# Splitting q and k for two heads at a time, and V once per unit, in a float16-split attention kernel

## The chip, the cores and the metric

The kernel runs on one core of a Trainium2 chip. The metric is the time of one execution on the device in microseconds. The engines named are PE (TensorE matmul; PEld is its weight load), DVE (VectorE), ACT (ScalarE), POOL (GpSimd) and SP (SyncE, which here only issues DMAs).

## The reference

Banded attention with a distance bias is followed by a two-layer feed-forward block (FF) on the same tokens. A query sees the 8 global keys and the 96 keys up to and including its own.

```python
# q, k, v: 4 batches, 8 heads, 768 tokens, 64 wide
scores = np.matmul(q, k.transpose(0, 1, 3, 2)) / np.sqrt(D)
keep = is_global | is_local            # key < 8, or 0 <= rel < 96
scores = np.where(keep, scores - slopes * dist, -1e9)
a = softmax(scores)
x = (a @ v) -> (3072, 512)
h = x @ w_in                           # 512 -> 2048
g = np.maximum(h, 0) + alpha * np.minimum(h, 0)
out = g @ w_out                        # 2048 -> 512
```

## The kernel before

The 3072 tokens are cut into 12 units `u` of 256 tokens, three to a batch. The first unit of a batch looks at three blocks of 128 keys, the others at four: for each of a unit's two query blocks its own 128 keys, and a far block of the 96 keys ahead of it and 32 leading keys of the batch. So the score window of a query block is 256 keys wide, and 128 for the first block of a batch. `windows` lists them.

Attention of unit `u` runs while the FF of the unit or two ahead of it uses PE. Units 0 to 2 attend in float32 (`plain`), while the weights are loaded and split. From unit 3 on every operand is split into a float16 high part and a float16 remainder. `mul` makes the high part (on ACT, DVE or POOL, as the planner chooses), `rest` makes the remainder (on DVE). For each head `attend` does this:

- one DMA brings `raw`, 128 partitions of q, k and V, 928 columns (736 in the first unit of a batch). The 64 rows of q and of k stand in it twice, in partitions 0 to 63 and again in 64 to 127 (L612).
- `q2` holds q's high part above and its remainder in the lower 64 partitions, `khi` and `klo` hold k's two parts, each twice (L622 to L625). So the two products of 128 rows at L656, `q2` with `khi` and `q2` with `klo`, sum all four cross terms.
- `vhi` and `vlo` split the head's V blocks (L631 to L641), far blocks included.
- DVE adds the bias `D` and takes a maximum (L662), ACT takes the exponential (L667), ACT or DVE and DVE split the probabilities into `ps` (L713, L714), an SP DMA transposes them into `pt` (L718), and PE multiplies them with V (L733), for two heads one behind the other.

FF of unit `u` and slice `f` (16 slices): twelve products of 256 columns into PSUM `h` (L795), activation on ACT and DVE into `g` (L343, L816, L818, L367), then per token block three products of 512 columns into `o` (L835). After the last slice ACT scales `o` into `os` (L842), an SP DMA stores it, and the two `o` buffers serve the next unit.

The order of instructions is fixed when the kernel is built. `Plan` keeps every operation with a key (its due slot), a cost and its buffers, runs a list schedule with the slots that `BUFS` gives to each tag, and emits the operations in the order of their planned start. On the chip each engine, SP's queue too, runs its own list strictly in that order. One FF slice is one step of the key. Scores of a head have the key of its place, the splits of q and k stand `KP` = 2 ahead of it, those of V one behind. `raw`, `q2`, `khi` and `klo` have two buffers each, PSUM `sp` and `h` have two.

Of the kernel before, what the change touches and what calls it, by code (L numbers as in the profile page):

```python
# [15 lines left out]
F16 = mybir.dt.float16  # L16
# [7 lines left out]
P = 128  # L24
# [22 lines left out]
def lay_out(q, k, v, n_global, n_local, moe_w_in, moe_w_out, moe_alpha):  # L47
# [6 lines left out]
    qk = np.zeros((2, 4, P, 672), q.dtype)  # L54
    vw = np.zeros((2, P, H * 256), q.dtype)
    for u in range(NU):
# [32 lines left out]
        "in_qkv_dram": qkv,  # L89
        "in_first0_dram": np.concatenate([qk[0, :, :, :544], vw[0, :, : H * 192].reshape(P, 4, 384).transpose(1, 0, 2)], axis=2),  # L90
        "in_first1_dram": cont(qk[1]),
        "in_first1v_dram": cont(vw[1].reshape(P, 2, 1024).transpose(1, 0, 2)),
# [200 lines left out]
NPLAIN = (8, 8, 8)  # L293
# [11 lines left out]
PT4 = 0  # L305
DL = 3
PREQ = (2,)
PREV = (2,)
PREP = (2,)
# [6 lines left out]
VLEAD = 22  # L316
# [3 lines left out]
BUFS = dict(rw=17, raw=2, q2=2, khi=2, klo=2, vhi=3, vlo=3, pr=2, sm=6, pt=2, ps=2, xn=1, xt=2, g=3, gh=3, gl=3,  # L320
# [3 lines left out]
def fast(tc, cn, a):  # L324
    nc = tc.nc
    ctx = ExitStack()
    with ctx:
# [218 lines left out]
        def load_first(u, h, key):  # L546

            x = buf("rw", f"first{u}_{h}", [P, 1024])
            nk, n = (672, 672) if u else (544, 928)

            def load():
                nc.sync.dma_start(out=x.t[:, :n], in_=a["first1" if u else "first0"][h // 2])
                if u == h == 0:
                    cn["load_alpha"]()
# [31 lines left out]

        def attend(u, h, key):

            b, c = divmod(u, 3)
            nk = 416 if c else 288  # L590
            nb = 4 if c else 3
            nv, npr = 64 * nb, 128 * nb
            plain = u < 3 and h < NPLAIN[u]
            uh = f"{u}_{h}"

            kp = key - KP
            if plain:

                if u < 2:
                    q2, qk_ = first[u, h]  # L600
                    rv, vrt = firstv[u, h]
                else:
                    q2 = rv = buf("raw", "raw" + uh, [P, 928])
                    op("SP", kp - 4, c_dma(P * 4 * (256 + nk + nv)), lambda: nc.sync.dma_start(
                        out=q2.t[:, : 256 + nk + nv], in_=a["qkv"][u, :, h, : 256 + nk + nv]), w=[q2])
                    qk_ = lambda: q2.t[:64, : 256 + nk]
                    vrt = lambda: q2.t[:, 256 + nk : 256 + nk + nv]
                q_ = lambda: qk_()[:, :256]
                keys = [(q2, lambda: qk_()[:, 256:])]
            else:  # L610
                raw = buf("raw", "raw" + uh, [P, 928])
                op("SP", kp - 4, c_dma(P * 4 * (256 + nk + nv)), lambda: nc.sync.dma_start(  # L612
                    out=raw.t[:, : 256 + nk + nv], in_=a["qkv"][u, :, h, : 256 + nk + nv]), w=[(raw, 0), (raw, 1)])
                rq, rv = (raw, 0), (raw, 1)
                rawt = lambda: raw.t
                vrt = lambda: raw.t[:, 256 + nk : 256 + nk + nv]
                q2 = buf("q2", "q2_" + uh, [P, 256], F16)
                q_ = lambda: q2.t
                khi = buf("khi", "khi" + uh, [P, 416], F16)
                klo = buf("klo", "klo" + uh, [P, 416], F16)  # L620
                kk = lambda: rawt()[:, 256 : 256 + nk]
# [4 lines left out]
                if (u, h) == (3, 0):  # L626
                    for x in range(H):
                        op("POOL", kp, c_pool(384, 1), lambda x=x: nc.gpsimd.tensor_scalar(
                            out=Dh[x].t, in0=Dh[x].t, scalar1=QS * QS, scalar2=None, op0=ALU.mult), w=[Dh[x]])
                keys = [(khi, lambda: khi.t), (klo, lambda: klo.t)]  # L630
            if not plain:  # L631
                vhi = buf("vhi", "vhi" + uh, [P, 256], F16)
                vlo = buf("vlo", "vlo" + uh, [P, 256], F16)
                vv = lambda: vrt()[:, :nv]
                if u in PREV:
                    mul(kp + 3, vv, vv, vs[b], [vs[b]], [rv], "ACT", nv)
                    copy(kp + 3, lambda: vhi.t[:, :nv], vv, [rv], [vhi], nv)
                    rest(kp + 3, lambda: vlo.t[:, :nv], vv, None, lambda: vhi.t[:, :nv], [rv, vhi], [vlo], nv, "POOL")
                else:
# [3 lines left out]
            sp = buf(idle(u, h, "sp", "h"), "sp" + uh, [P, 512])  # L643
# [7 lines left out]
            def scores():  # L651
                if (u, h) == (1, 0):
                    keep_busy(sp.t)
                for qb, off, n, _, pc in windows(u):
                    for j, (_, kk) in enumerate(keys):
                        nc.tensor.matmul(sp.t[:, pc : pc + n], lhsT=q_()[:, 128 * qb : 128 * qb + 128],  # L656
                                         rhs=kk()[:, off : off + n], start=j == 0, stop=j == len(keys) - 1)

            cost = (2 * npr * 0.84 if plain else 0.852 * npr)
            op("PE", key, cost, scores, r=[q2] + [x for x, _ in keys], w=[sp])  # L660
# [26 lines left out]
            if plain:  # L687
# [11 lines left out]
                prods = lambda: ((pt.t, vrt()),)  # L699
                used = [pt, rv]  # L700
                cost = 207 * nb
            else:
                ps = buf("ps", "ps" + uh, [P, 2, 512], F16)
                pt = buf("wf" if PT4 and u > 2 else "pt", "pt" + uh, [P, 2, 512], F16)
# [3 lines left out]
                if u in PREP:  # L708
                    mul(key + 2, pp, pp, PSC, [], [pr], "ACT", npr)
                    copy(key + 2, p0, pp, [pr], [(ps, 0)], npr)  # L710
                    rest(key + 2, p1, pp, None, p0, [pr, (ps, 0)], [(ps, 1)], npr, "POOL")
                else:
                    mul(key + 2, p0, pp, PSC, [pr], [(ps, 0)], "ACT", npr)  # L713
                    rest(key + 2, p1, pp, PSC, p0, [pr, (ps, 0)], [(ps, 1)], npr)  # L714
# [7 lines left out]
                prods = lambda: ((pflat(), vhi.t), (pflat(), vlo.t), (pflat()[:, npr:], vhi.t))  # L722
# [324 lines left out]
```

## Time and profile before

| | |
|---|---|
| median of 3 runs | 657.1 us (656.23 to 658.21) |
| the profiled execution | 655.59 us, of which the span is 653.8 us |
| PE busy | 624.0 us of the span (95%) |
| DVE, ACT, POOL busy | 518.0, 406.8, 129.1 us |
| granted TensorE clock | 0.997 over the span |
| DMA | 92.9 MB moved, 63.1 MB of it read from HBM |

The matmul records overlap and their ends are modelled, so that a PE which is called busy may still lose time. What a product costs is therefore read from one start to the next.

### The profile page before, as it was taken

The numbers are of one execution on the slowest core, as the hardware profiler recorded it, in microseconds if no ns is written. First come the engines' busy times: TensorE is split into PE (matmuls) and PEld (weight loads), VectorE is DVE, ScalarE is ACT, GpSimd is POOL, SyncE is SP. The second block draws the span as 40 slices with busy tenths as digits, with TensorE's granted clock in tenths as the row PEclk, the third lists the DMA queues.
The fourth block names the chain that finished last, engine by engine and source line by source line (L and its number), as shares of the span: only waits on it lengthen the run. The fifth ranks groups of instructions, "written<-read, shape, count | busy, mean of one in ns | idle before, by whom it ended". The sixth has DMA issues, their size and how long they took to land.

```text
span 653.8 us, 13833 instructions
## 1 busy us (share of the span) xinstructions
PE 624.0 (95%) x4964; PEld 438.0 (67%) x4964; DVE 518.0 (79%) x1497; ACT 406.8 (62%) x1085; POOL 129.1 (20%) x185
## 2 busy tenths in 40 slices
PE   8998998999999999899899999999899999999995
PEld 7785666675666666576567676676576677676663
DVE  6899999868888899877989887877988888874331
ACT  6998866536756666766666665673656666653332
POOL 1003342212222223112222122111222112100000
PEclk9999999999999999999999999999999999999998
DMA  8998311115747546843656647764666646621001
GB/s 307 403 406 330 102 59 60 59 55 152 179 103 172 148 105 129 236 116 92 136 151 139 188 102 126 204 155 63 171 156 124 172 133 125 167 47 38 33 1 39
DMA packets 115807, 92.90 MB, mean 142 GB/s; under 512 B 93968, under 2 KB 93968, under 8 KB 115728
## 3 DMA queue, kind: packets, MB, share of 16 engines
q1 hardware_dynamic: 115728, 91.91, 52.1%
q8 instruction: 41, 0.67, 0.4%
q14 instruction: 38, 0.31, 0.2%
HBM read 63.06 MB, written 6.29 MB: 106 GB/s over the span
## 4 chain that ended last, share of the span: by engine, by line
PE 33%; DVE 30%; DMA 20%; ACT 11%; issue 4%; POOL 1%; SPq 0%; ACTq 0%; DVEq 0%; POOLq 0%
DMA raw<-in_qkv_dram 15%; PE o L835 13%; PE h L795 13%; ACT pr L667 4%; DVE ps L368 4%; DVE g L816 3%; DVE klo L368 3%; PE sp L656 3%; DVE q L368 2%; DVE vlo L368 2%; PE av L733 2%; DMA xt<-xs 2%; DMA vr<-in_v_dram 2%; DVE pr L662 2%; DVE vhi L344 2%
## 5 line engine op out<-in xcount | busy, mean ns | idle before, releaser
L795 PE MATMUL h<-xt,whl 128*128 128x256 f16 x2304 | 281.2, 273 | 1.6 <-DVE g L816 1.2
L795 PEld LDWEIGHTS <-whl 128*128 128x128 f16 x2304 | 224.6, 98 | 63.4 <-issue 3.0
L835 PE MATMUL o<-whl,g 128*128 128x512 f16 x864 | 215.6, 379 | 5.4 <-ACT os L842 5.3
L835 PEld LDWEIGHTS <-g 128*128 128x128 f16 x864 | 82.6, 98 | 71.6 <-issue 8.1
L367 POOL TENSOR_TENSOR g<-g 128x256 f16<-128x256 f32 x88 | 67.9, 773 | 256.5 <-ACT g L818 254.1
L667 ACT ACTIVATE pr<-pr,sm 128x256 f32<-128x256 f32 (+1 forms) x192 | 92.7, 484 | 34.9 <-DVE sm L662 34.5
L343 ACT ACTIVATE g<-h,ak 128x256 f32<-128x256 f32 x167 | 77.9, 467 | 55.2 <-PE h L795 52.6
L816 DVE SCALAR_TENSOR_TENSOR g<-h,g 128x256 f32<-128x256 f32 x192 | 80.0, 418 | 32.4 <-ACT g L343 32.0
L818 ACT CAST g<-g 128x256 f16<-128x256 f32 x144 | 57.1, 399 | 59.0 <-DVE g L816 58.6
L662 DVE CUSTOM_DVE_ANT_0 pr<-sp,D 128x256 f32<-128x256 f32 (+1 forms) x192 | 71.3, 393 | 3.5 <-PE sp L656 2.7
L368 DVE SCALAR_TENSOR_TENSOR ps<-pr,ps 128x512 f16<-128x512 f32 (+1 forms) x72 | 49.0, 680 | 12.9 <-ACT ps L343 12.6
L835 PE MATMUL o<-whl,gh 128*128 128x512 f16 x192 | 57.2, 379 | 0.7 <-ACT gh L818 0.6
L367 POOL TENSOR_TENSOR gl<-g,gh 128x256 f16<-128x256 f32 x32 | 30.2, 945 | 110.2 <-ACT gh L818 99.2
L368 DVE SCALAR_TENSOR_TENSOR klo<-raw,khi 128x416 f16<-128x416 f32 (+1 forms) x72 | 43.6, 605 | 1.8
L835 PE MATMUL o<-whl,gl 128*128 128x512 f16 x96 | 36.5, 380 | 2.4 <-POOL gl L367 2.0
L368 DVE SCALAR_TENSOR_TENSOR q<-raw,q 64x256 f16<-64x256 f32 x72 | 32.8, 455 | 6.8 <-ACT q L343 3.9
L367 DVE TENSOR_TENSOR g<-g 128x256 f16<-128x256 f32 x56 | 23.8, 425 | 16.5 <-ACT g L818 16.3
L656 PE MATMUL sp<-klo,q 128*128 128x256 f16 (+1 forms) x144 | 34.0, 263 | 2.3 <-DVE klo L368 2.3
L667 ACT ACTIVATION_READ_ACCUMULATOR pr<-pr,sm 128x1 f32 x192 | 36.2, 189 | 0.0
L733 PEld LDWEIGHTS <-pt 128*128 128x128 f16 x792 | 28.4, 98 | 11.3 <-DMA pt<-ps 3.5
L368 DVE SCALAR_TENSOR_TENSOR vlo<-raw,vs,vhi 128x256 f16<-128x256 f32 (+1 forms) x72 | 35.8, 517 | 0.1
L656 PE MATMUL sp<-khi,q 128*128 128x256 f16 (+1 forms) x144 | 33.8, 264 | 2.1 <-DVE sm L662 1.3
(122 smaller groups left out, 734.6 us busy)
## 6 DMA issues: line engine op xcount, KB each, us to landing
raw<-in_qkv_dram SPq DMA_DIRECT2D x56, 464.0 KB, 3.9
w<-in_w_dram SPq DMA_DIRECT2D x32, 512.0 KB, 9.0
raw<-in_qkv_dram SPq DMA_DIRECT2D x24, 368.0 KB, 3.4
out_dram<-os SPq DMA_DIRECT2D x24, 256.0 KB, 2.4
vr<-in_v_dram SPq DMA_DIRECT2D x18, 256.0 KB, 4.0
first<-in_first_dram SPq DMA_DIRECT2D x4, 464.0 KB, 5.3
vr<-in_v_dram SPq DMA_DIRECT2D x3, 512.0 KB, 8.4
first<-in_first_dram SPq DMA_DIRECT2D x4, 336.0 KB, 10.1
```

The costliest lines, as they stand in the source:

```text
L343: lambda: nc.scalar.mul(out=out(), in_=src(), mul=by.t if tile_ else by)),
L344: DVE=("DVE", c_dve(n, not psum, tile_), lambda: v.tensor_scalar(out=out(), in0=src(), scalar1=by.t if tile_ else by, scalar2=None, op0=AL ...
L367: return e.tensor_tensor(out=out(), in0=src(), in1=hi(), op=ALU.subtract)
L368: return e.scalar_tensor_tensor(out=out(), in0=src(), scalar=val(), in1=hi(), op0=ALU.mult, op1=ALU.subtract)
L656: nc.tensor.matmul(sp.t[:, pc : pc + n], lhsT=q_()[:, 128 * qb : 128 * qb + 128], rhs=kk()[:, off : off + n], start=j == 0, stop=j == len( ...
L662: op("DVE", key, c_dve(n) + 10, lambda qb=qb, n=n, dc=dc, pc=pc: v.tensor_tensor_reduce(out=pr.t[:, pc : pc + n], in0=sp.t[:, pc : pc + n] ...
L667: op("ACT", key + 1, c_act(n, ptr=1) + 93, lambda qb=qb, n=n, pc=pc: nc.scalar.activation(out=pr.t[:, pc : pc + n], in_=pr.t[:, pc : pc + ...
L733: nc.tensor.matmul(out, lhsT=p_[:, 128 * j : 128 * j + 128], rhs=v_[:, 64 * j : 64 * j + 64], start=m == 0, stop=m == len(ps) - 1)
L795: nc.tensor.matmul(hp.t, lhsT=w.t[:, wi, wc], rhs=x.t[:, NC * xi + c, :], start=n == 0, stop=n == 3 * NC - 1)
L816: op("DVE", key, c_dve(UT), lambda: v.scalar_tensor_tensor(out=g_(), in0=hp.t, scalar=KG, in1=g_(), op0=ALU.mult, op1=ALU.max), r=[hp], w= ...
L818: op("ACT", key, c_act(UT), lambda: nc.scalar.copy(out=gh_(), in_=g_()), r=[rg], w=[rh])
L835: nc.tensor.matmul(o.t, lhsT=g_()[:, tok], rhs=w.t[:, wi, 512:1024], start=f == 0 and n == 0, stop=f == NF - 1 and n == 2)
```

## The change

From unit 3 on one DMA brings q and k of two heads (`load_pair`): head 0 of the pair in partitions 0 to 63, head 1 in 64 to 127, 672 columns (544 in the first unit of a batch). One `mul` and one `rest` split all of it into `x16`. The scores are products of 64 rows: high with high, high with remainder, remainder with high, for the two heads in turn, each head into an `sp` buffer of its own; the product of the two remainders is left out. `load_v` brings the 256 tokens of V of a unit once, for all heads, splits them into `v16`, and SP's queue copies the rows of the far blocks from `v16` of this unit or the one ahead, and the leading rows from `gp` of the one ahead, into `gp`. The products with V (now L761) read `v16` and `gp`. Unit 2 keeps its float32 products, and reads the paired layout that units 0 and 1 had.

```diff
-BUFS = dict(rw=17, raw=2, q2=2, khi=2, klo=2, vhi=3, vlo=3, pr=2, sm=6, pt=2, ps=2, xn=1, xt=2, g=3, gh=3, gl=3,
+BUFS = dict(rw=17, raw=3, x16=3, pr=2, sm=6, pt=2, ps=2, xn=1, xt=2, g=3, gh=3, gl=3,
...
-VLEAD = 22
+VLEAD = 26.5
+VS = 5
+VL = 4
...
+        def load_v(u, key):
+            b, c = divmod(u, 3)
+            raw = buf("rw", f"vraw{u}", [P, 1024])
+            x = v16[u] = buf("rw", f"v16_{u}", [P, 1024])
+            g = gp[u] = buf("rw", f"gp{u}", [P, 1024])
...
+            for j in range(2):
...
+                mul(k, hi, in_, vs[b], [raw, vs[b]], [(x, (j, 0))], "ACT", 512)
+                rest(k, lo, in_, vs[b], hi, [raw, vs[b], (x, (j, 0))], [(x, (j, 1))], 512)
+            key += VS + 1
...
+            if c:
+                move(0, "0p", 0, GL, P, v16[u - 1], 1, ((1, 0), (1, 1)))
+                move(0, "0g", LOC, LOC, P, gp[u - 1], 1, ("1g",))
+                move(1, "1g", LOC, LOC, P, gp[u - 1], 1, ("1g",))
+            else:
+                move(1, "1g", LOC, 0, GL, x, 0, ((0, 0), (0, 1)))
+            move(1, "1p", 0, GL, P, x, 0, ((0, 0), (0, 1)))
...
+        def load_pair(u, h, key):
...
+            op("SP", key - KP - 4, c_dma(P * 4 * n), lambda: nc.sync.dma_start(
+                out=raw.t[:, :n], in_=a["qk"][u - 1, h // 2, :, :n]), w=[raw])
...
+            mul(key - KP, hi, lambda: raw.t[:, :n], QS, [raw], [(x, 0)], n=n)
+            rest(key - KP, lo, lambda: raw.t[:, :n], QS, hi, [raw, (x, 0)], [(x, 1)], n)
...
+            def scores():
+                for qb, off, m, _, pc in windows(u):
+                    for j, (qi, ki) in enumerate(((0, 0), (0, 1), (1, 0))):
+                        for i, sp in enumerate(sps):
+                            rows = slice(64 * i, 64 * i + 64)
+                            nc.tensor.matmul(sp.t[:, pc : pc + m], lhsT=x.t[rows, qi, 128 * qb : 128 * qb + 128],
+                                             rhs=x.t[rows, ki, 256 + off : 256 + off + m], start=j == 0, stop=j == 2)
+            op("PE", key, 3 * 0.426 * (512 if u % 3 else 384) + 300, scores, r=[x], w=sps)
...
-                mul(kp, lambda: q2.t, lambda: rawt()[:, :256], QS, [rq], [q2], n=256)
-                mul(kp, lambda: khi.t[:, :nk], kk, QS, [rq], [khi], n=nk)
-                rest(kp, lambda: q2.t[64:, :], lambda: rawt()[64:, :256], QS, lambda: q2.t[64:, :], [rq], [q2], 256)
-                rest(kp, lambda: klo.t[:, :nk], kk, QS, lambda: khi.t[:, :nk], [rq, khi], [klo], nk)
...
-                    mul(kp + 3, lambda: vhi.t[:, :nv], vv, vs[b], [rv, vs[b]], [vhi], "DVE", nv)
-                    rest(kp + 3, lambda: vlo.t[:, :nv], vv, vs[b], lambda: vhi.t[:, :nv], [rv, vs[b], vhi], [vlo], nv)
...
+            if u > 2:
+                jobs.append((begin(u) - VL, load_v, (u,)))
```

The change moves the order on every engine. Three places show it.

PE, where unit 7 scores its first heads behind FF slice 10 of unit 5 (`sp7_0` is the score buffer of unit 7, head 0). Before:

```order
L795 MATMUL h5_10_4936<-xt5_4296,whl10_1349 128x256
L656 LDWEIGHTS q2_7_0_4864
L656 MATMUL sp7_0_4954<-khi7_0_4866,q2_7_0_4864 128x256
L656 LDWEIGHTS q2_7_0_4864
L656 MATMUL sp7_0_4954<-klo7_0_4894,q2_7_0_4864 128x256
L656 LDWEIGHTS q2_7_0_4864
```

Now, at the same FF slice:

```order
L823 MATMUL h5_10_4695<-xt5_4188,whl10_1356 128x256
L648 LDWEIGHTS x16_7_0_4229
L648 MATMUL sp7_0_4709<-x16_7_0_4229 128x256
L648 LDWEIGHTS x16_7_0_4229
L648 MATMUL sp7_1_4711<-x16_7_0_4229 128x256
L648 LDWEIGHTS x16_7_0_4229
```

Before, four loads and products of one head stand here (the two further ones are those of the second window), and head 1 follows two slices later. Now twelve loads and products of heads 0 and 1 in turn stand here, and the next pair follows four slices later.

ACT, at the end of the FF of unit 3, where `os3_0` frees the first of the two `o` buffers (`g4_1` is unit 4's activation of slice 1, `q2_5_5` the high part of q of unit 5, head 5). Before:

```order
L667 ACTIVATE pr5_3_3747,sm5_2_3627<-pr5_3_3747,sm5_2_3627 128x256 x2
L343 ACTIVATE ps5_3_3767<-pr5_3_3747 128x512
L343 ACTIVATE g4_1_3775<-h4_1_3751,ak_158 128x256
L343 ACTIVATE q2_5_5_3784<-raw5_5_3739 128x256
L842 ACTIVATE os3_0_3801<-o3_0_3052,osc1_2071 128x512
L818 CAST g4_1_3775<-g4_1_3775 128x256
```

Now:

```order
L339 ACTIVATE g4_1_3630<-h4_1_3613,ak_146 128x256
L846 CAST g4_1_3630<-g4_1_3630 128x256
L870 ACTIVATE os3_0_3650<-o3_0_2975,osc1_1874 128x512
L339 ACTIVATE g4_2_3668<-h4_2_3637,ak_146 128x256
L339 ACTIVATE x16_6_2_3677<-raw6_2_3177 128x544
L846 CAST g4_2_3668<-g4_2_3668 128x256
L870 ACTIVATE os3_1_3687<-o3_1_3006,osc1_1874 128x512
```

Before, the split of `raw5_5` stands just ahead of `os3_0`. Now no split stands ahead of it; behind it comes that of `raw6_2`, a pair of the unit after.

SP, where unit 7's first probabilities are transposed (`pt7_0`) and `xt6`, unit 6's FF input, is made. Before:

```order
L718 DMA_TRANSPOSE pt7_0_5028<-ps7_0_4996 128x8x128
L612 DMA raw7_3_5056<-in_qkv_dram 128x928
L763 DMA_TRANSPOSE xt6_5066<-xs6_0_5049 128x8x128
L763 DMA_TRANSPOSE xt6_5066<-xs6_1_5053 128x8x128
L612 DMA raw7_4_5103<-in_qkv_dram 128x928
L718 DMA_TRANSPOSE pt7_1_5132<-ps7_1_5098 128x8x128
L718 DMA_TRANSPOSE pt7_2_5224<-ps7_2_5184 128x8x128
L612 DMA raw7_5_5248<-in_qkv_dram 128x928
L612 DMA raw7_6_5255<-in_qkv_dram 128x928
```

Now:

```order
L605 DMA gp7_4768<-v16_6_4137 96x1024
L605 DMA gp7_4768<-gp6_4158 32x1024 x2
L739 DMA_TRANSPOSE pt7_0_4803<-ps7_0_4760 128x8x128
L605 DMA gp7_4768<-v16_7_4725 96x1024
L630 DMA raw8_4_4835<-in_qk_dram 128x672
L791 DMA_TRANSPOSE xt6_4841<-xs6_0_4824 128x8x128
L791 DMA_TRANSPOSE xt6_4841<-xs6_1_4827 128x8x128
L739 DMA_TRANSPOSE pt7_1_4870<-ps7_1_4805 128x8x128
L630 DMA raw8_6_4948<-in_qk_dram 128x672
```

Before, the loads in this stretch are of unit 7 itself, heads 3 to 6. Now they are pairs of unit 8, and the four copies into `gp7` stand between, the last of them behind `pt7_0` and ahead of `xt6`.

## Rows read from the trace of the kernel before

**Rows 1.** Part 1 of the page: busy time of PE, PEld, DVE, ACT and POOL over the span, share, and number of instructions.

```profile
PE 624.0 (95%) x4964; PEld 438.0 (67%) x4964; DVE 518.0 (79%) x1497; ACT 406.8 (62%) x1085; POOL 129.1 (20%) x185
```

**Rows 2.** Busy time of each engine from 146 to 600 us, where units 3 to 11 attend in float16 (ahead of it units 0 to 2 attend in float32 while the weights come in). The columns are the stage, its length, then for PE, PEld, DVE, ACT and POOL the busy us and the number of instructions, the granted clock, the DMA share and GB/s.

```profile
146.00:600.00 454.00, 439.12 (x3707) 305.51 (x3705) 374.77 (x1104) 283.88 (x775) 94.77 (x145) 1.00 0.58 138
```

**Rows 3.** The timeline of PE in a stretch without a wait. The columns are the start in us, how long the piece lasts to its modelled end, engine, line, operation, tiles, shape, count. Each piece starts before the modelled end of the one ahead, so rates are read from start to start.

```profile
337.30 1.47 PE L795 MATMUL h<-xt,whl 128*128 128x256 f16 x12
338.61 0.27 PE L656 MATMUL sp<-khi,q 128*128 128x256 f16 x1
...
339.05 1.46 PE L835 MATMUL o<-whl,g 128*128 128x512 f16 x6
340.35 1.47 PE L795 MATMUL h<-xt,whl 128*128 128x256 f16 x12
```

**Rows 4.** The timeline of PE in a group of 24 products with V (L733), of which the second head's twelve begin at 404.56. In brackets stands the idle time before the piece and what ended it.

```profile
403.15 0.19 PE L733 MATMUL av<-vhi,pt 128*128 128x64 f16 x1
404.56 0.20 PE L733 MATMUL av<-vhi,pt 128*128 128x64 f16 x1 [1.21 <-DMA pt<-ps]
...
404.92 0.81 PE L835 MATMUL o<-whl,g 128*128 128x512 f16 x3
```

**Rows 5.** The stage of 146 to 600 us for the instructions of one line at a time: L795 (first FF product), L835 (second FF product), L656 (scores), L733 (probabilities times V), in this order. The columns are as in rows 2, with PE and PEld alone.

```profile
146.00:600.00 454.00, 212.98 (x1740) 169.85 (x1740) 1.00 0.58 138
146.00:600.00 454.00, 219.76 (x881) 83.06 (x879) 1.00 0.58 138
146.00:600.00 454.00, 42.13 (x288) 25.87 (x288) 1.00 0.58 138
146.00:600.00 454.00, 29.93 (x792) 28.39 (x792) 1.00 0.58 138
```

**Rows 6.** Who PE (first four rows) and PEld (last two) waited for in 146 to 600 us: us in total, times, longest.

```profile
PE o L835 <- ACT os L842: 5.3, 7, 2.2
PE av L733 <- DMA pt<-ps: 2.9, 5, 1.2
PE sp L656 <- DVE klo L368: 2.3, 8, 0.5
PE sp L656 <- DVE sm L662: 1.3, 2, 0.8
...
PEld L656 <- issue: 5.1, 10, 1.1
PEld L656 <- DVE q L368: 3.3, 8, 0.8
```

**Rows 7.** The longest wait of PE in this stage, in the timeline of PE.

```profile
262.14 0.59 PE L835 MATMUL o<-whl,g 128*128 128x512 f16 x2
264.95 0.38 PE L835 MATMUL o<-whl,g 128*128 128x512 f16 x1 [2.21 <-ACT os L842]
```

**Rows 8.** ACT at the time of rows 7, in its timeline.

```profile
262.17 0.46 ACT L343 ACTIVATE g<-h,ak 128x256 f32<-128x256 f32 x1
263.91 0.42 ACT L343 ACTIVATE q<-raw 128x256 f16<-128x256 f32 x1 [1.28 <-DMA raw<-in_qkv_dram]
264.23 0.67 ACT L842 ACTIVATE os<-o,osc 128x512 f32<-128x512 f32 x1
```

**Rows 9.** ACT at the time of the wait in rows 4, in its timeline.

```profile
403.68 0.42 ACT L343 ACTIVATE q<-raw 128x256 f16<-128x256 f32 x1 [3.02 <-DMA raw<-in_qkv_dram]
```

**Rows 10.** The view of one tile, `raw` (the loaded q, k and V of a head): the first row stands under the heading of idle time of the engines before its instructions (us, times) until the thing named; the last under the heading of who waited for it.

```profile
  DMA raw<-in_qkv_dram: 64.6, 71
...
  ACT q L343: 24.1, 23
```

**Rows 11.** The timeline of PE around 64-row float32 score products: one head alone between two FF products, and two heads one behind the other, whose operands lie in partitions 0 to 63 and 64 to 127 (last two rows). Each float32 product leaves two records, so 4 records are one head and 8 are two. The rows at 66.72 and 66.94 are the same four records from the second and from the third on.

```profile
66.09 0.38 PE L835 MATMUL o<-whl,gl 128*128 128x512 f16 x1
66.40 1.13 PE L656 MATMUL sp<-raw 64*128 64x256 f32 x4
...
66.72 0.81 PE L656 MATMUL sp<-raw 64*128 64x256 f32 x3
66.94 0.59 PE L656 MATMUL sp<-raw 64*128 64x256 f32 x2
...
67.46 0.28 PE L795 MATMUL h<-xt,whl 128*128 128x256 f16 x1
...
24.45 1.14 PE L656 MATMUL sp<-first 64*128 64x256 f32 x8
25.52 0.33 PE L771 MATMUL xp<-ident,xn 128*128 128x128 f32 x1
```

**Rows 12.** Weight loads of the first FF product among the page's groups (busy us, mean ns), and, from the page's DMA issues, the load of one head (count, KB each, median us from issue to landing).

```profile
L795 PEld LDWEIGHTS <-whl 128*128 128x128 f16 x2304 | 224.6, 98 | 63.4 <-issue 3.0
...
raw<-in_qkv_dram SPq DMA_DIRECT2D x56, 464.0 KB, 3.9
```

**Rows 13.** From the page's groups and from the groups by shape: the low halves of the splits on DVE, with busy us and mean ns of one, and last one group of a width of 512.

```profile
L368 DVE SCALAR_TENSOR_TENSOR klo<-raw,khi 128x416 f16<-128x416 f32 (+1 forms) x72 | 43.6, 605 | 1.8
L368 DVE SCALAR_TENSOR_TENSOR q<-raw,q 64x256 f16<-64x256 f32 x72 | 32.8, 455 | 6.8 <-ACT q L343 3.9
L368 DVE SCALAR_TENSOR_TENSOR vlo<-raw,vs,vhi 128x256 f16<-128x256 f32 (+1 forms) x72 | 35.8, 517 | 0.1
L368 DVE SCALAR_TENSOR_TENSOR ps<-pr,ps 128x512 f16<-128x512 f32 x48 | 33.2, 692 | 12.7 <-ACT ps L343 12.6
```

More of the change, by code (lines that the diff above doesn't have):

```diff
@@ L289, in c_dma @@
     return nbytes / 360.0
-NPLAIN = (8, 8, 8)
 V0 = -70
@@ L546, in load_first @@
         def load_first(u, h, key):
-            x = buf("rw", f"first{u}_{h}", [P, 1024])
+            x = buf("rw", f"first{u}_{h}", [P, 1024]) if u < 2 else buf("raw", f"first{u}_{h}", [P, 672])
             nk, n = (672, 672) if u else (544, 928)
             def load():
-                nc.sync.dma_start(out=x.t[:, :n], in_=a["first1" if u else "first0"][h // 2])
+                nc.sync.dma_start(out=x.t[:, :n], in_=a["qk"][u - 1, h // 2] if u else a["first0"][h // 2])
                 if u == h == 0:
@@ L587, in attend @@
         def attend(u, h, key):
             b, c = divmod(u, 3)
-            nk = 416 if c else 288
             nb = 4 if c else 3
-            nv, npr = 64 * nb, 128 * nb
-            plain = u < 3 and h < NPLAIN[u]
+            npr = 128 * nb
+            plain = u < 3
             uh = f"{u}_{h}"
-            kp = key - KP
             if plain:
[L599 to L609, printed above, removed]
-            else:
[L611 to L621, printed above, removed]
-                mul(kp, lambda: q2.t, lambda: rawt()[:, :256], QS, [rq], [q2], n=256)
-                mul(kp, lambda: khi.t[:, :nk], kk, QS, [rq], [khi], n=nk)
-                rest(kp, lambda: q2.t[64:, :], lambda: rawt()[64:, :256], QS, lambda: q2.t[64:, :], [rq], [q2], 256)
-                rest(kp, lambda: klo.t[:, :nk], kk, QS, lambda: khi.t[:, :nk], [rq, khi], [klo], nk)
[L626 to L630, printed above, removed]
@@ L643, in attend @@
-            sp = buf(idle(u, h, "sp", "h"), "sp" + uh, [P, 512])
+                if u == 2 and h % 2 == 0:
+                    load_first(u, h, key - KP - 4)
+                q2, qk_ = first[u, h]
+                rv, vrt = firstv[u, h]
+                sp = buf(idle(u, h, "sp", "h"), "sp" + uh, [P, 512])
+            else:
+                if h % 2 == 0:
+                    load_pair(u, h, key)
+                sp = pair[u, h]
             pr = buf(idle(u, h, "pr", "stage"), "pr" + uh, [P, 512])
@@ L654, in scores @@
                 for qb, off, n, _, pc in windows(u):
[L655 to L660, printed above, removed]
+                    nc.tensor.matmul(sp.t[:, pc : pc + n], lhsT=qk_()[:, 128 * qb : 128 * qb + 128],
+                                     rhs=qk_()[:, 256 + off : 256 + off + n], start=True, stop=True)
+            if plain:
+                op("PE", key, 2 * npr * 0.84, scores, r=[q2], w=[sp])
             for qb, _, n, dc, pc in windows(u):
@@ L707, in attend @@
                 p0, p1 = (lambda: sflat()[:, :npr]), (lambda: sflat()[:, npr : 2 * npr])
[L708 to L714, printed above, removed]
+                mul(key + 2, p0, pp, PSC, [pr], [(ps, 0)], "ACT", npr)
+                rest(key + 2, p1, pp, PSC, p0, [pr, (ps, 0)], [(ps, 1)], npr)
                 def transposes():
```

78 lines of the change are left out of this document (49 added, 29 removed).

## Prediction

> **What bounds the kernel now.** I read part 1 of the page first: PE is busy for 624.0 of 653.8 us, DVE for 518.0, ACT for 406.8 [rows 1]. So PE is the bound, and the question is what PE loses. The table of stages puts the change where it acts. From 146 to 600 us, where the attention of units 3 to 11 runs, PE is busy for 439.1 of 454 us, DVE for 374.8, ACT for 283.9 [rows 2]. The modelled ends hide part of the loss, so I count it from starts. In a stretch without a wait twelve L795 products take 1.31 us from start to start, 0.109 each; the score products of one head take 0.44, so also 0.109; six L835 products take 1.30, 0.216 each [rows 3]. Twelve L733 products take 0.36, 0.030 each [rows 4]. With the counts of this stage [rows 5] that is 1740 x 0.109 = 189.7, 881 x 0.216 = 190.3, 792 x 0.030 = 23.8, and for the 288 score products 28.8 (240 of 256 columns, and 48 of 128, taken at half). The sum is 432.6. PE loses about 21 us of the 454.
>
> The list of waits says where. PE waits 5.3 us for `os`, 2.9 for transposed probabilities, 3.6 for the remainder of k and for the readers of the score buffer; its weight loads wait 5.1 and 3.3 us ahead of scores [rows 6]. About 7 of the 21 us stand at scores. The other waits look unrelated, and two timelines show that they are not. In the longest one PE stands for 2.21 us until `os` [rows 7]; ACT then sits 1.28 us in front of the split of q, until its DMA lands, and only behind that split does `os` start, at 264.23 [rows 8]. The `ACT` order shows why: `q2_5_5` stands ahead of `os3_0`. The longest wait for transposed probabilities is 1.21 us at 404.56 [rows 4], and ACT had just been idle for 3.02 us in front of a `raw` [rows 9]. The view of the tile `raw` sums this up: the engines were idle for 64.6 us, 71 times, until a `raw` landed, ACT 24.1 of it at q alone [rows 10]. With two `raw` buffers of one head each, a load is issued when the head two places ahead is done with V, and its user stands at the front of an engine that also feeds FF.
>
> **What the change does, part by part.**
>
> *Score products.* Before, a head with two windows of 256 takes 4 x 0.109 = 0.436, a pair 0.872. Now a pair issues twelve products of 64 rows. Whether two heads run side by side decides this part. The float32 units show it: one head alone (4 records) takes 1.06 us, 66.40 to 67.46, and two heads in different halves (8 records) take 1.07 us, 24.45 to 25.52 [rows 11]. They overlap fully. So a pair streams 6 x 0.109 = 0.654, and 3 x (0.109 + 0.055) = 0.49 where the first window is 128 wide (before 0.656 a pair). With 24 and 12 pairs that is 24 x -0.218 + 12 x -0.166 = -7.2 us.
>
> *Changing between 128 and 64 rows.* The same rows price it. The last FF product starts at 66.09, and at 0.216 the next one could follow at 66.31; it starts at 67.46, 1.15 us later. The records follow each other by 0.22 (66.72, 66.94), so four stream in 0.87, twice 0.109 each, and going in and out costs 0.28 us. Before, scores in float16 had nothing of this [rows 3]. 36 pairs x 0.28 = +10.1 us. I take that whole. From below it is +6.5 us: on each side a start is late by 0.09 (66.40 for 66.31), 0.18 a pair, and the rest is the first step at 66.40, 0.32 long, where float32 weights come in. PE's own work thus changes by +2.9 us (-0.7 from below). On PE alone the change is a small loss.
>
> *Where a rule speaks against it.* In the trace twelve L795 products with twelve weight loads of 98 ns [rows 12] take 1.31 us [rows 3], so the loads are hidden behind products on the same rows. The Trainium skill, TensorE: Matmul & The Clock Gate, Part 3, says that a weight load overlaps running products only when its row group differs. By that rule each product of a head would wait for its load, the third rival below. The trace disagrees with it for 128 rows; no row shows 64-row float16.
>
> *q and k.* A pair's load has 344 KB (279 KB) in place of 2 x 464 [rows 12], three of them are held, and three `x16`. `raw` is now freed by its split and not by V. The SP order shows the result: around `pt7_0` it issues loads of unit 8, where before it issued those of unit 7. A load then lands tens of us ahead of its split, against a landing time of 3.9 us [rows 12]. The 64.6 us of waits [rows 10] should go nearly to zero.
>
> *DVE.* The remainders of klo, q and vlo take 43.6 + 32.8 + 35.8 = 112.2 us [rows 13]. In their place stand 24 splits of 672 columns, 12 of 544 and 18 of 512. From 692 ns at 512 [rows 13] I estimate 0.91, 0.74 and 0.69: 21.8 + 8.9 + 12.4 = 43 us. DVE loses some 69 us and the high halves besides, but it was idle for 79 us of the stage already, so this is worth nothing by itself; it makes PE's suppliers earlier.
>
> *V.* One load of 512 KB, two high and two low halves, and two to four copies a unit. I cost them at nothing on PE. A copy's nearest row is a `raw` load of 464 KB, 3.9 us [rows 12]; it is issued ahead of the transposes of head 1, without which the first products with V cannot start either. Without this cover a late copy costs PE its whole landing, 3.9 us a unit.
>
> *A new wait.* A pair needs both `sp` buffers at once. Pairs stand four FF slices apart, and a slice takes 1.31 + 1.30 us [rows 3], so the four reads have 10 us. Behind the pair DVE and ACT get the work of two heads in one piece. I leave that inside the waits that remain.
>
> *Up to 146 us.* Units 0 to 2 keep their products. I take no change, and 2 us either way for the loads of unit 2 that now stand among the weights.
>
> **The sum.** Of the 21 us I take away the 7 at scores, 3 of the 5 at `os`, 2 at transposed probabilities, and nothing else: -12. With +2.9 that is -9.1. The bounds are -20 (all waits go, lower price of the change of rows) and -2 (only the waits at scores go, part of them coming back where a pair waits for both buffers). The profiled execution took 655.6 us, 1.8 over its span; 655.6 - 9.1 = 646.5. The median of the runs stands 1.5 above the profiled one, so **648.0**.
>
> **Rivals.**
>
> 1. *The waits have other causes.* `os` comes at each unit's end, when ACT has the new unit's activations too; that speaks for it, the wait for a landing ahead of `os` against it [rows 8]. Then only 4 to 7 us go, against 2.9: -1 to -4, 653 to 656.
>
> 2. *SP's order turns into the wait.* The copy from `v16_7` stands ahead of `xt6`, FF's next input. If DVE's split of V is late, SP stands at that copy and with it `xt6`, and PE waits at the unit's first L795. It decides once the split ends later than the end of `xs6`, which is planned behind it on DVE; that speaks against it. Two us in each of nine units give back 18: 648 + 18 = 666.
>
> 3. *64-row float16 products do not overlap, or wait for their weights.* In turn, a pair takes 1.31 + 0.28 against 0.872, 24 times, and 0.98 + 0.28 against 0.656, 12 times: +17.2 + 7.2 = +24 in place of +2.9, so 648 + 21 = 669. With a load of 98 ns [rows 12] ahead of each of six steps it is 36 x 0.59 = +21, 669. The overlap in float32 [rows 11] speaks against both. The second form is the one that the rule of the Trainium skill named above would give.
>
> 4. *Nearly all waits go.* 637 to 642. The two timelines [rows 8, 9] speak for it, the remaining kinds of waits [rows 6] against.
>
> **Chances.** Forecast (642 to 653) 0.63; rival 1 0.18; rival 2 0.07; rival 3 0.07; rival 4 0.05. A difference under 0.3%, 2 us, is about what a measurement of this kernel can't tell from none. Rival 1 lies half on each side of that line, so faster is 0.63 + 0.05 + 0.10 = 0.78, same 0.09 with the rest of it; slower is 0.13, rivals 2 and 3 but for 0.01. The range for 8 in 10 is 641 to 657: the forecast, rival 1 and part of rival 4. It leaves out rivals 2 and 3.
>
> **What the profile would show.** Right: no `raw` among the waits of ACT and DVE; twelve score products in 0.9 to 1.0 us from the last FF product ahead to the next one behind, with starts in couples; DVE below 450 us (518 - 69); a loss of PE near 10 us in the float16 stage. Wrong: score products that start 0.109 apart one by one (rival 3); PE waiting at L795 for `xt` (rival 2); waits at `os` as before (rival 1). The forecast fails most easily on the price of changing rows, which is paid 36 times, and on how many of the `os` waits belong to `raw`.

## The result, and the profile after

The changed kernel takes 641.3 us (640.6 to 643.4, 4 runs), the kernel before on the same chip 656.9 (656.2 to 658.2, 4 runs): a ratio of 0.977 (95% interval 0.974 to 0.979), 15.6 us less. I had predicted 648.0, in a range of 641 to 657: the time lies at the lower edge of the range. The profiled execution took 641.4 us, 14.2 less than that of before.

Part 1 of the page after, and the first row of the chain that ended last (before, PE had 33% of that chain, DVE 30%, DMA 20%):

```profile
PE 620.6 (97%) x5108; PEld 427.3 (67%) x5108; DVE 448.2 (70%) x1280; ACT 384.6 (60%) x1006; POOL 112.5 (18%) x157
...
PE 81%; DVE 9%; DMA 3%; issue 3%; ACT 2%; POOL 1%; SPq 0%; POOLq 0%; DVEq 0%; ACTq 0%
```

DVE is busy for 70 us less, and PE now makes up 81% of that chain. The stage of 146 to 600 us, in the columns of [rows 2], then for the lines L823 (first FF product, L795 before), L863 (second, L835 before), L648 (scores) and L761 (probabilities times V, L733 before):

```profile
146.00:600.00 454.00, 451.45 (x3977) 306.28 (x3976) 308.16 (x893) 267.16 (x710) 76.18 (x114) 1.00 0.49 108
...
146.00:600.00 454.00, 224.01 (x1833) 178.96 (x1833) 1.00 0.49 108
146.00:600.00 454.00, 227.52 (x916) 84.31 (x915) 1.00 0.49 108
146.00:600.00 454.00, 28.21 (x432) 16.81 (x432) 1.00 0.49 108
146.00:600.00 454.00, 29.14 (x792) 28.08 (x792) 1.00 0.49 108
```

In the same 454 us PE now gets through 93 more products of L823 and 35 more of L863 than in [rows 5]. By the rates of the prediction they are 1833 x 0.109 + 916 x 0.216 + 792 x 0.030 = 421.5 us, and 36 pairs of scores stream 21.6. That is 443.1, so PE loses 10.9 us where it lost 21.

Who PE waited for in this stage, all of it ([rows 6] before), and what the view of `raw` has in place of [rows 10]:

```profile
PE h L823 <- DVE g L844: 2.0, 3, 0.8
PE av L761 <- DMA pt<-ps: 0.3, 1, 0.3
PE sp L648 <- DVE sm L688: 0.2, 1, 0.2
```

```profile
its engine sat idle before it (us, times) until:
  PE sp L648: 3.8, 16
who waited for it (us, times):
```

The waits for `os` are gone wholly, those for transposed probabilities nearly, and no engine waits for a landing of `raw`.

One pair of scores in PE's timeline, which has no wait in it, and the same place again in two narrow windows, which show how many products have started by 331.95 and by 332.06:

```profile
331.90 0.83 PE L648 MATMUL sp<-x 64*128 64x256 f16 x12
332.66 0.82 PE L863 MATMUL o<-whl,g 128*128 128x512 f16 x3
...
331.70 0.27 PE L823 MATMUL h<-xt,whl 128*128 128x256 f16 x1
331.90 0.28 PE L648 MATMUL sp<-x 64*128 64x256 f16 x2
...
331.90 0.39 PE L648 MATMUL sp<-x 64*128 64x256 f16 x4
```

Two products start together, the next two 0.11 us later. From the last FF product ahead (331.70) to the next one behind (332.66) it is 0.96 us; without the 0.109 of that FF product and 0.654 of streaming, 0.20 remain for going in and out of 64 rows. All but two of the 36 pairs give 0.20 to 0.21 in this way; the two have a further delay inside.

A loss stands early, in unit 2's attention:

```profile
107.39 0.38 PE L863 MATMUL o<-whl,gl 128*128 128x512 f16 x1
110.30 0.63 PE L719 MATMUL tp<-ident,pr 128*128 128x128 f32 x4 [2.53 <-DVE xn L770]
110.76 2.07 PE L823 MATMUL h<-xt,whl 128*128 128x256 f16 x12
112.76 2.07 PE L682 MATMUL sp<-first 64*128 64x256 f32 x4
```

The same place in two stretches, in the columns of [rows 2]:

```profile
107.00:110.30 3.30, 0.77 (x5) 0.18 (x3) 3.30 (x8) 1.60 (x4) 1.16 (x2) 1.00 0.01 2
110.30:118.20 7.90, 7.90 (x35) 5.00 (x36) 5.67 (x13) 5.33 (x13) 2.53 (x2) 0.57 0.25 73
```

PE stands until DVE has written `xn` of two heads of unit 2, and in the 7.9 us behind the wait (last row) the granted clock is 0.57: twelve FF products take 2.00 us from start to start in place of 1.31, so part of this stretch ran at 1.2 GHz in place of 2.4. Counted over the starts of L823 in both traces, the first FF product of unit 1 comes 0.7 us later than before, the middle of unit 1 4.6 later, the first product of unit 2 3.0 later (154.7 against 151.8), and the first of unit 11 14.3 earlier (586.0 against 600.3). So 17.2 us are gained behind 152 us, and 3 are lost ahead of it.

### The profile page after: what moved, and what is told of

Its sections match the earlier page's. It is cut to its first block, busy times and chain, and to the rows that moved or that the text cites. A ratio compares the mean times of both kernels' runs of the same rounds, so it can differ in the third digit from the quotient of the medians.

```text
span 639.2 us, 13816 instructions
## 1 busy us (share of the span) xinstructions
PE 620.6 (97%) x5108; PEld 427.3 (67%) x5108; DVE 448.2 (70%) x1280; ACT 384.6 (60%) x1006; POOL 112.5 (18%) x157
## 4 chain that ended last, share of the span: by engine, by line
PE 81%; DVE 9%; DMA 3%; issue 3%; ACT 2%; POOL 1%; SPq 0%; POOLq 0%; DVEq 0%; ACTq 0%
PE h L823 35%; PE o L863 34%; PE av L761 5%; PE sp L648 4%; PE sp L682 2%; DMA first<-in_first_dram 1%; DVE pr L688 1%; PE tp L719 1%; POOL gl L363 1%; DVE wf L532 1%; DVE v L364 1%; DVE wb L529 1%; DVE whl L364 1%; DMA gp<-v 1%; DMA xt<-xs 1%
## 5 line engine op out<-in xcount | busy, mean ns | idle before, releaser
L823 PE MATMUL h<-xt,whl 128*128 128x256 f16 x2304 | 283.5, 274 | 2.4 <-DVE g L844 2.0
L823 PEld LDWEIGHTS <-whl 128*128 128x128 f16 x2304 | 225.3, 98 | 66.8 <-issue 5.7
L863 PE MATMUL o<-whl,g 128*128 128x512 f16 x864 | 215.2, 379 | 0.0
L863 PEld LDWEIGHTS <-g 128*128 128x128 f16 x864 | 80.0, 98 | 70.3 <-issue 6.9
L363 POOL TENSOR_TENSOR g<-g 128x256 f16<-128x256 f32 x63 | 47.2, 748 | 274.7 <-ACT g L846 274.6
L688 DVE CUSTOM_DVE_ANT_0 pr<-sp,D 128x256 f32<-128x256 f32 (+1 forms) x192 | 66.7, 396 | 4.1 <-PE sp L682 3.6
L363 DVE TENSOR_TENSOR g<-g 128x256 f16<-128x256 f32 x81 | 34.4, 424 | 35.2 <-ACT g L846 35.2
L863 PE MATMUL o<-whl,gh 128*128 128x512 f16 x192 | 57.7, 382 | 0.1
L363 POOL TENSOR_TENSOR gl<-g,gh 128x256 f16<-128x256 f32 x31 | 29.2, 945 | 93.0 <-ACT gh L846 81.5
L863 PE MATMUL o<-whl,gl 128*128 128x512 f16 x96 | 36.5, 380 | 2.1 <-POOL gl L363 2.0
L761 PEld LDWEIGHTS <-pt 128*128 128x128 f16 x792 | 28.1, 98 | 7.9 <-DMA pt<-ps 0.4
L364 DVE SCALAR_TENSOR_TENSOR x<-raw,x 128x672 f16<-128x672 f32 (+1 forms) x36 | 33.3, 926 | 0.0
L863 PEld LDWEIGHTS <-gh 128*128 128x128 f16 x192 | 18.1, 100 | 15.8 <-issue 1.8
L846 ACT CAST gh<-g 128x256 f16<-128x256 f32 x48 | 19.1, 398 | 15.6 <-PE o L863 8.1
L706 POOL TENSOR_TENSOR fin<-fin,sm 128x4 f32<-128x4 f32 x36 | 15.3, 425 | 74.3 <-ACT pr L693 72.9
L648 PE MATMUL sp<-x 64*128 64x256 f16 (+1 forms) x432 | 28.2, 262 | 0.2 <-DVE sm L688 0.2
```

Of the source, the lines that this page charges most:

```text
L363: return e.tensor_tensor(out=out(), in0=src(), in1=hi(), op=ALU.subtract)
L364: return e.scalar_tensor_tensor(out=out(), in0=src(), scalar=val(), in1=hi(), op0=ALU.mult, op1=ALU.subtract)
L648: nc.tensor.matmul(sp.t[:, pc : pc + m], lhsT=x.t[rows, qi, 128 * qb : 128 * qb + 128], rhs=x.t[rows, ki, 256 + off : 256 + off + m], star ...
L688: op("DVE", key, c_dve(n) + 10, lambda qb=qb, n=n, dc=dc, pc=pc: v.tensor_tensor_reduce(out=pr.t[:, pc : pc + n], in0=sp.t[:, pc : pc + n] ...
L706: op("POOL", key + 3, c_pool(2 * G), lambda: nc.gpsimd.tensor_tensor(out=fin.t, in0=fin.t, in1=sm.t[:, 2 * G : 4 * G], op=ALU.add), r=[(sm ...
L761: nc.tensor.matmul(out, lhsT=p_[:, 128 * j : 128 * j + 128], rhs=v_(j), start=m == 0, stop=m == len(ps) - 1)
```

## Experiments

Theory A is that of the prediction: loads of q and k land late, and engines that wait for them in order hold up PE's suppliers. Theory B, the rival: DVE's shorter work is the gain. Ratios are to the kernel before on the same chip; "counted over starts" means the first FF products of units 2 and 11, as above.

**Earlier loads alone.** The kernel before with one number changed.

```diff
-BUFS = dict(rw=17, raw=2, q2=2, ...
+BUFS = dict(rw=17, raw=3, q2=2, ...
```

> The kernel before with one number changed: three buffers for raw in place of two. Loads can be issued one head earlier, nothing else of the change is in it: DVE keeps its 518 us, scores keep 128 rows. Theory A (the gain is the end of the waits for raw): most of the 64.6 us for which engines were idle in front of a raw go (under 15 left), PE loses 9 to 14 us less after 146 us, the time is 643 to 649 against 657. Theory B (the gain is DVE's shorter work): no more than 3 us, 654 to 659, whatever becomes of the waits for raw.

Measured: 647.1 us against 659.5, ratio 0.983 (0.980 to 0.986). Counted over starts, 12.6 us are gained from unit 2 to unit 11. This row of the view of `raw` stands for the 64.6 us of [rows 10]:

```profile
  DMA raw<-in_qkv_dram: 15.4, 12
```

DVE was busy for 509.7 us, hardly less than before. The waits left are at the edge of what was expected (under 15). That speaks for A, and leaves some 5 us to explain.

**Loads of q and k apart from V.** Still the kernel before, with every split as it was.

```diff
-BUFS = dict(rw=17, raw=2, q2=2, ...
+BUFS = dict(rw=17, raw=3, rawv=3, q2=2, ...
...
-                raw = buf("raw", "raw" + uh, [P, 928])
+                raw = rq = buf("raw", "raw" + uh, [P, 672])
+                rv = buf("rawv", "rawv" + uh, [P, 256])
```

> The kernel before with its load cut in two: q and k of a head in raw (672 columns, three buffers, freed by their split), V of a head in a tile of its own (256 columns, three buffers, issued three slots later). Each head still splits its own q, k and V blocks, with the same instructions as before: DVE keeps its 510 to 518 us. before_raw3 left 15.4 us of idle time in front of raw and lay 5 us above v_once_only. Theory A in its strict form (late loads are all of it): these waits go too and the time falls to that of v_once_only, 640 to 644, 15 us or more below the kernel before. Rival (V split once removes work from the queues of DVE, ACT and POOL in front of the transposed probabilities, and that is the rest): 645 to 649, as before_raw3, with PE still waiting 3 us or more in the products with V.

Measured: 642.8 us against 661.6, ratio 0.975 (0.968 to 0.982). Part 1 of its page, then its row in the view of `raw`:

```profile
PE 619.6 (97%) x4964; PEld 439.3 (69%) x4964; DVE 505.1 (79%) x1434; ACT 430.3 (67%) x1149; POOL 135.4 (21%) x184
```

```profile
  DMA raw<-in_qkv_dram: 0.2, 1
```

Its stage of 146 to 600 us, and all that PE waited for there (L738 is V, L800 and L840 are FF):

```profile
146.00:600.00 454.00, 451.81 (x3836) 319.17 (x3834) 363.30 (x1039) 310.64 (x841) 99.92 (x143) 1.00 0.65 137
```

```profile
PE av L738 <- DMA pt<-ps: 1.4, 1, 1.4
PE h L800 <- DVE g L821: 0.5, 1, 0.5
PE o L840 <- ACT os L847: 0.3, 1, 0.3
```

From unit 2 to unit 11 it gains 18.3 us, as much as the changed kernel (17.2), with DVE at 505 us, products of 128 rows and V split for each head. The waits at scores, at `os` and half of those at V belonged to the late loads. This is theory A in its strict form, with one thing that the edit did not hold still: the planner, which picks the engine of each high half, gave ACT 133 of those of q and k (85 before), so the order and the engines moved with the loads. That the lighter DVE is not what helped, the next run shows; what the new order is worth without the earlier loads was not run.

**DVE's work given back.**

```diff
-            rest(key - KP, lo, lambda: raw.t[:, :n], QS, hi, ...)
+            for _ in range(2):
+                rest(key - KP, lo, lambda: raw.t[:, :n], QS, hi, ...)
```

and the same for the low halves of V.

> The changed kernel with each low half of q and k and of V written twice, one behind the other: DVE gets 43 us of work back, some 490 in all, nothing else changes. Theory A: PE does not wait for DVE, the time is that of the changed kernel within 2 us. Theory B (DVE's shorter work is the gain): 43 of 69 us of DVE are given back and with them some 9 us, 650.

```profile
PE 618.3 (97%) x5108; PEld 426.6 (67%) x5108; DVE 480.7 (75%) x1306; ACT 392.0 (61%) x1020; POOL 122.9 (19%) x171
```

Measured: 641.3 us, ratio 0.976 (0.971 to 0.982); the changed kernel on the same chip had 641.2. DVE got 32.5 us back in the records, less than the 43 expected, as the planner moved some of its other work to POOL and ACT. Nothing of it reached the time: from unit 2 to unit 11 the gain is 17.1 us, in the changed kernel 17.2. Theory B falls.

> The changed kernel once more, so that the three runs beside it, and v_once_only through its ratio to the kernel before, have it on the same chip: 641, 15 to 16 us below the kernel before (ratio 0.974 to 0.979).

Measured: 641.2 us against 656.9, ratio 0.972 (0.966 to 0.977), a little below the ratios expected. The time goes with the clock: three executions took 641.2 to 641.3 us at a mean granted clock of 0.990 or 0.991, two took 636.5 and 637.4 at 0.996 and 0.997.

**V once, without the pairing of heads.** `load_pair` is replaced by the loads and splits of before for q and k (`q2`, `khi`, `klo`, four products of 128 rows a head), with three buffers of 672 columns.

> The changed kernel with q and k taken back to the way of before (one head at a time, products of 128 rows, q2, khi and klo), so that V split once per unit is the part of the change that stays; raw holds q and k of one head and has three buffers, and is freed by its split. Theory A: the loads land early here too, so the waits go, and PE's own work differs from that of the changed kernel by 7.2 us more streaming and no change of rows, 36 x 0.20 = 7.2 us less: the time is that of the changed kernel, 639 to 645. Had I been right to price a change of rows at 0.28 us, it would be 3 us below the changed kernel. Theory B (DVE): DVE gets back 76 of the 100 us of low halves (its busy time near 490), and the time goes more than halfway back, 649 to 655.

Measured: 640.9 us, ratio 0.969 (0.965 to 0.974); 17.6 us gained from unit 2 to unit 11, DVE 480.1 us. The pairing moves no time that these runs can tell (the changed kernel gains 17.2 and, in changed_again, 17.6 us there): what PE streams less, it pays for the change of rows.

**The price of changing rows, paid more often.**

```diff
-            op("PE", key, ..., scores, r=[x], w=sps)
+            for w in range(2):
+                op("PE", key + w, ..., lambda w=w: scores(w), r=[x], w=[(y, w) for y in sps])
```

> The changed kernel with the twelve score products of a pair cut into two groups of six, one for each window, due one FF slice apart, so that PE changes between 128 and 64 rows 72 times in place of 36. By the price that the trace of the changed kernel shows (0.20 us to go in and out) the time is 36 x 0.20 = 7.2 us above the changed kernel, 648 to 649; by the price that my prediction took, 0.28, it is 10 us above, 651 to 652. If a change of rows costs nothing that its neighbours don't hide: 641 to 643.

Measured: 649.3 us, ratio 0.982 (0.977 to 0.987), against 0.972 to 0.977 for the changed kernel. From unit 2 to unit 11 it gains 8.1 us in place of 17.2: 9 lost, of which some 1.5 are waits for transposed probabilities and others that the changed kernel has not. The trace has 67 groups of scores, not 72, as five pairs still ran both windows in one go: 31 changes more than 36, which is 6.2 us at 0.20 and 8.7 at 0.28. The 7.5 us left lie between, so the total does not decide between the two prices. A group in PE's timeline does:

```profile
383.98 0.38 PE L864 MATMUL o<-whl,g 128*128 128x512 f16 x1
384.29 0.50 PE L648 MATMUL sp<-x 64*128 64x256 f16 x6
384.73 0.39 PE L864 MATMUL o<-whl,g 128*128 128x512 f16 x1
```

It is 0.75 us from the FF product ahead to the next one; without the 0.216 of that FF product and 0.327 for three couples, 0.20 remain here too.

**The order of the two heads.**

```diff
-                for qb, off, m, _, pc in windows(u):
-                    for j, (qi, ki) in enumerate(((0, 0), (0, 1), (1, 0))):
-                        for i, sp in enumerate(sps):
+                for i, sp in enumerate(sps):
+                    for qb, off, m, _, pc in windows(u):
+                        for j, (qi, ki) in enumerate(((0, 0), (0, 1), (1, 0))):
```

> The changed kernel with the same twelve score products of a pair in another order: first all six of head 0, then all six of head 1. If two heads overlap only where neighbours in PE's order lie on different halves of the rows, a pair takes 12 x 0.109 + 0.20 = 1.51 us in place of 0.86 in 24 pairs, and 0.98 + 0.20 in place of 0.69 in 12: 24 x 0.65 + 12 x 0.49 = +21 us, 662. If, besides, a 64-row product waits for a load of its own rows of 98 ns (the rule of the Trainium skill, TensorE: Matmul & The Clock Gate, Part 3, would have it so), the products start 0.207 apart and 36 x 12 x 0.098 = 42 us come on top, 704. If PE finds the overlap in any order: 641.

Measured: 648.1 us (643.5 to 651.3), ratio 0.981 (0.977 to 0.985). None of the three numbers. The profiled execution had its first FF product 4.0 us later than the others, before any changed work (from 12 to 22 us its granted clock is 0.51, in the changed kernel 1.00). From unit 2 to unit 11 it gains 10.0 us where the changed kernel gains 17.2, so 7.2 us are lost, not 21. PE's timeline over one pair, and how many products have started by 337.30, 337.45 and 337.56:

```profile
337.27 1.06 PE L648 MATMUL sp<-x 64*128 64x256 f16 x12
338.27 0.39 PE L863 MATMUL o<-whl,g 128*128 128x512 f16 x1
...
337.27 0.28 PE L648 MATMUL sp<-x 64*128 64x256 f16 x1
...
337.27 0.39 PE L648 MATMUL sp<-x 64*128 64x256 f16 x2
...
337.27 0.52 PE L648 MATMUL sp<-x 64*128 64x256 f16 x4
```

One, two, then four: the third and the fourth begin 8 ns apart (337.503 and 337.511), and from there on there are two chains with steps of 0.109. The records of the two products that end a head (they signal DVE) start at 337.83 and 338.07, so the chain that began at 337.27 is head 0 and the one from 337.51 is head 1. PE took head 1's products ahead of head 0's fourth, fifth and sixth, which stand before them in the program. The pair takes 1.00 us from 337.27 to 338.27 in place of 0.76. A pair whose first window is 128 wide, in the changed kernel and then here:

```profile
320.25 0.67 PE L648 MATMUL sp<-x 64*128 64x128 f16 x12
320.85 0.82 PE L863 MATMUL o<-whl,g 128*128 128x512 f16 x3
...
325.49 0.80 PE L648 MATMUL sp<-x 64*128 64x128 f16 x12
326.22 0.60 PE L863 MATMUL o<-whl,g 128*128 128x512 f16 x2
```

That is 0.73 us in place of 0.60, and 24 x 0.234 + 12 x 0.127 = 7.1, the whole of the loss.

**Late loads in the changed kernel.** `raw` gets one buffer, and the load of a pair a place behind the pair ahead's last transposes in SP's order.

> The changed kernel with one buffer for raw, and each pair's load placed in SP's order behind the transposes of the probabilities of the pair ahead, so that loads are issued as late as a raw freed by its V was before. PE's products, DVE's and ACT's work stay. Theory A: engines are idle in front of a raw for over 20 us in all, and 4 to 10 us of the gain are lost: 645 to 652 against 641. Theory B (DVE): 641, 2 us either way.

Measured: 723.3 us, ratio 1.097. Engines were idle for 19.8 us in front of a `raw`, close to what was expected, but the time is far off. Who PE waited for from 146 to 700 us:

```profile
PE h L823 <- DMA xt<-xs: 21.9, 10, 5.5
PE sp L648 <- DVE x L340: 13.3, 5, 3.1
PE sp L648 <- DVE x L364: 8.6, 11, 2.2
```

With the load behind the transposes each pair's load, split, scores and softmax stand in one chain with the next pair's; the attention of a unit outlasts its 16 slices, and PE waits for the next unit's `xt`. The granted clock, 0.942 over the span, is down as well. The run shows that a load which comes late enough costs this kernel much; it was too large a change to say anything on the size of the effect in the kernel before.

**The early loss.** Unit 2's four writes of `xn` (`soon`) are moved to right behind the products that they read.

```diff
         out = sorted(range(n), key=lambda i: (start[i], i))
+        for i in self.soon:
+            out.remove(i)
+            out.insert(max(out.index(j) for j in ops[i][2]) + 1, i)
```

> The changed kernel with unit 2's four writes of xn on DVE moved forward in the order, each to right behind the products that it reads (the second of them by five places, ahead of four operations of the weights' split and one of FF). Nothing else is changed. In the changed kernel PE stood for 2.7 us at 107.4 us until this write was done, and the products between 111 and 118 us then ran at half the granted clock. Theory C (the early loss is the place of this write): the stall falls to under 0.5 us, the clock stays, 4 to 6 us are gained: 635 to 638. Rival (DVE is busy without a gap from 60 to 112 us, so whatever goes ahead delays a split weight by as much, and PE waits there): 640 to 642.

Measured: 638.0 us (median; the changed kernel beside it 641.2), ratio 0.971 (0.965 to 0.976). The intervals of the two ratios overlap, and 3.2 us are less than the 4 to 6 expected. The traces of the two profiled executions, this one and that of changed_again, differ where they should: both have the first FF product at 29.2 us, and the first of unit 2 at 151.0 against 154.7. PE in the same place, and the two stretches:

```profile
108.50 0.38 PE L870 MATMUL o<-whl,gl 128*128 128x512 f16 x1
108.72 0.60 PE L724 MATMUL tp<-ident,pr 128*128 128x128 f32 x4
109.15 1.47 PE L830 MATMUL h<-xt,whl 128*128 128x256 f16 x12
```

```profile
107.00:110.30 3.30, 3.30 (x27) 2.51 (x26) 3.30 (x7) 1.70 (x5) 1.73 (x2) 1.00 0.02 7
110.30:118.20 7.90, 7.90 (x56) 5.52 (x55) 7.87 (x20) 6.84 (x16) 3.43 (x3) 1.00 0.24 71
```

No wait, and the clock stays at 1.00. Of the 3.7 us, 2.8 are left at the end. So the wait is a matter of order on DVE: the earlier loads of unit 2 let DVE's reading of later scores (`pr`) slip ahead of `xn`. DVE's timeline before, and in the changed kernel:

```profile
108.50 0.41 DVE L742 TENSOR_TENSOR xn<-av,sm 128x256 f32<-128x256 f32 x1
113.59 0.41 DVE L662 CUSTOM_DVE_ANT_0 pr<-sp,D 128x256 f32<-128x256 f32 x1
...
104.86 0.40 DVE L688 CUSTOM_DVE_ANT_0 pr<-sp,D 128x256 f32<-128x256 f32 x1
109.74 0.41 DVE L770 TENSOR_TENSOR xn<-av,sm 128x256 f32<-128x256 f32 x1
```

before_raw3 and before_v_apart, whose loads come earlier too, have a like wait (3.13 us from start to start at 111), and in both the clock stayed at 1.00 behind it. What the wait costs hangs on the clock. Two executions of changed_again, with the wait's order in place, took 636.5 and 637.4 us at a high clock, no longer than xn2_sooner.

> The kernel of v_once_only (V split once, q and k one head at a time with 128 rows) with the same moving of unit 2's xn. It tells whether the pairing of heads is worth anything on PE with the early loss out of both: by theory A (36 x 0.20 for the change of rows against 7.2 us less streaming) it is within 1 us of xn2_sooner. If the shorter work of DVE counts (480 against 448 us), it is 2 or more slower.

Measured: 637.0 us (636.0 to 639.6), ratio 0.969 (0.964 to 0.974), the lowest median of all, and about 1 us below xn2_sooner with 31 us more work on DVE (478.5 against 447.0).

## Why the prediction was right in direction and short in size

- **PE is the bound, and late `raw` loads are behind what it loses.** Right. before_v_apart shows it with nothing edited but the loads; the order and the engines that the planner then chose went with them.
- **The waits that go: -12.** Too small; this is the term that failed. Of 21 us that PE lost, the changed kernel keeps 10.9, of which 7.2 are the new changes of rows: 3.7 of the old kind, so 17.3 went. I had followed the chain back to `raw` in two timelines, and then credited only 3 of the 5 us at `os`, 2 of those at V, and nothing that was not in the list of waits by name. In before_v_apart the counts of the stage (1836 x 0.109 + 922 x 0.216 + 23.8 + 280 x 0.100 = 451) leave a loss of 3. What I had priced as rival 4, at 5 in 100, is what happened. The sign "a loss of PE near 10 us" came true by luck: I meant 21 - 12 of old waits, with the changes of rows booked apart, and the 10.9 measured are 3.7 of old waits and 7.2 of row changes.
- **Streaming of the scores: -7.2.** Right: couples, 0.109 apart.
- **Changing rows: +10.1.** My lower bound, 6.5, was nearer. The trace has 0.20 us a pair, 7.2 in all. The 0.28 came from float32 rows [rows 11], where the first step is 0.32 long; here the first step is 0.12.
- **The rule against it.** A line of the Trainium skill, TensorE: Matmul & The Clock Gate, Part 3, lets a weight load run beside products only on another row group. Products of one head start 0.109 us apart with loads of 94 ns on the same 64 rows (heads_not_in_turn), so the trace disagrees with that line for 64 rows, as it did for 128. The same part of the Trainium skill also lets a load into the background weight buffer run ahead; that would fit, and no run here shows whether it is what happens.
- **Up to 146 us: nothing, 2 either way.** Wrong by a little: 2.7 us are lost, counted over starts with the start-up taken off. Some 2.4 of them are the clock, which fell behind a wait on DVE's order: dve_splits_twice, with the same wait and no fall, loses 0.3. I had looked at the loads of unit 2 only as traffic among the weights, not at what an earlier arrival does to DVE's order.
- **DVE's relief is worth nothing by itself, V costs nothing.** Right, by dve_splits_twice and v_once_only.
- **The sum.** -17.3 - 7.2 + 7.2 + 2.7 = -14.6, against -14.2 measured between the two profiled executions. Against the forecast of -9.1 the waits (5.3) and the changes of rows (2.9) both erred to the slow side, the start (2.7) to the fast side. The load of a pair has 336 or 272 KB in the unit of [rows 12], where I wrote 344 and 279; nothing hangs on it.

Rivals: the waits had no other cause (1); SP's order cost nothing, as no product waits for `xt` (2); the products of two heads overlap (3).

## What to carry to other kernels

When timelines tie several kinds of waits to one late transfer, take it that all of them belong to it and price the whole loss, not the named waits alone; then test it by changing only the load and when its buffer is freed, which here, with the order that the planner then chose, was worth the entire gain. Less work on an engine that was not the bound, and fewer columns paid for with more changes of rows, came to nothing here, so undo each part of a rewrite before you keep it. Earlier loads also move an ordered queue's other work ahead: look at who then stands behind it.

## What the runs showed of the hardware that I had not expected

- PE does not start products strictly in program order when they lie on different halves of the rows: in heads_not_in_turn head 1's first started 0.24 us after head 0's first, with three of head 0's still to come that stand ahead of it in the program. So what I wrote of the kernel before, that each engine runs its own list strictly in order, does not hold for PE here.
- Going from 128 to 64 rows and back cost 0.20 us for float16, about half of it on each side: in the changed kernel's pair the first score product starts 0.20 us after an FF product of 0.109 (331.70, 331.90), 0.09 late.
- The wait of 2.9 us from start to start at 107.4 is in dve_splits_twice as well, and there the clock did not fall:

```profile
110.30:118.20 7.90, 7.82 (x53) 5.48 (x54) 7.87 (x19) 6.29 (x15) 3.67 (x4) 1.00 0.23 63
```

Its first FF product of unit 2 came 2.4 us earlier than the changed kernel's, with the start-up taken off. Behind a wait of 2.5 to 3.1 us from start to start in this place the clock fell in the changed kernel, changed_again and v_once_only (0.57, 0.78 and 0.59 from 110.3 to 118.2 us), and not in dve_splits_twice, before_raw3 and before_v_apart. Why it fell in some executions and not in others stays open.
